# A retention layer with two gated feed-forward layers on one core: order of activations, splits, products and stores

## The chip, the core and the metric

The kernel runs on one NeuronCore of a Trainium2 chip. Five engines work there side by side, each through its own list of instructions, in the order of that list: TensorE (PE in the profile; its weight loads are shown apart as PEld), VectorE (DVE), ScalarE (ACT), GpSimd (POOL) and SyncE (SP), which here only issues transfers. An instruction starts when its engine has come to it and the semaphores that it waits for have arrived. The metric is the device time of one execution in microseconds (us), as the median of several executions.

## The reference

A retention layer (attention with a decay in place of the softmax) feeds two feed-forward layers. There are 4 batches of 576 positions, 8 heads of 64, hence 2304 tokens of 512 features; both feed-forward layers have 2048 hidden features.

```python
def _attn_ref(q, k, v):
    scores = scale * np.matmul(q, k.transpose(0, 1, 3, 2))
    Dmat = np.where(rel >= 0, gamma[:, None, None] ** rel[None, :, :], 0.0)
    return np.matmul(scores * Dmat[None], v)
def _moe_ref(x, w_in, w_out):          # layer 1
    h = x @ w_in
    g = h * np.tanh(softplus(h))
    return (g @ w_out).astype(np.float32)
def _moe2_ref(x, w_in, w_out):         # layer 2
    h = x @ w_in
    g = h * (1.0 / (1.0 + np.exp(-1.702 * h)))
    return (g @ w_out).astype(np.float32)
```

The weights of both layers come as 64-bit numbers, and all sums are wanted near float32 accuracy.

## The kernel before

**Split operands.** TensorE multiplies a shortened 32-bit format (`F32R`). Each operand of the two layers is therefore kept as a first part, rounded to that format, and a second part, the remainder; each product takes three matmuls (`PARTS`: first x first, first x second, second x first). The first part is one copy (on ScalarE through `act`, in some places on VectorE), the second part one VectorE subtraction that reads the first.

**Stage 1, retention** (to about 80 us). 20 units (batch, 128 positions) run one after another: `scores` (L738), `update` of the running state (L761), `outputs` (L786, L797), and `finish` (L811), which writes the result into the tile `X` of 512 features by 2304 columns. Between these calls stand jobs that turn the first weights of layer 1 from 64 bits into two parts (`convert`: VectorE L181, L126, L193, L234, ScalarE L117, GpSimd L197). GpSimd also scales each unit's `v` (L727). `split_x` makes the two parts of a block of columns of `X`, one 128-feature piece k at a time: first part by ScalarE for even k and by VectorE (L123) for odd k, then L333 on VectorE. In this stage it is called after the units listed in `X_UNITS`: four pieces of the first block (512 columns), then four of the side block (256 columns).

**Stage 2, layer 1** (80 to 477 us). The columns are cut into blocks; `SLOTS` lists (block, 128 hidden features) in order. The first block and the side block take turns (32 slots), then come blocks of 512 columns. At step i the program issues `up(i)` (12 matmuls, L346), `down(i - 3)` (12 matmuls, L367) and `elementwise(i)`: Mish of `h` on ScalarE into `c`, the first part of `g` on ScalarE, its second part on VectorE (L396), then jobs that convert layer 2's weights and write them to DRAM (`prepare`, on all engines). Where the next slot begins a new block, `elementwise` first calls `split_x` for all four pieces of it. The matmuls of a block's first slot are ordered so that 8 on first parts come ahead of 4 on second parts. `elementwise(0)` and `elementwise(1)` are already called in the last two units of stage 1, and the condition for a new block holds for slot 1, the side block's first.

**Stage 3, layer 2** (477 us to the end). A matrix product cut into quarters is made from seven products of sums of quarters instead of eight. Three rounds of 768 columns each have two halves. First half, "up" (L582): eight passes r, each with seven steps, one for each product p in the order `UP_ORDER`. After a step `combine` forms quarters of the hidden layer with VectorE (L428), and `after` gives a finished quarter (numbers 22, 11, 21, 12) to ScalarE for the Gelu, in place in the tile `cs` of that pass or out of a PSUM bank. Second half, "down" (L638): seven products in the order `DOWN_ORDER`, each with eight steps. A step is six matmuls in either half. `operand(i + AHEAD)`, called at the head of each step, makes the down operand that is needed three steps later: first part `g` by ScalarE, second part by VectorE (L428); the last three up steps already make operands for the first down steps. Weights come from DRAM through a ring of five tiles; `load_weights` issues each load on SyncE four tiles ahead. `leave` issues the stores of finished output quarters on SyncE.

Of the kernel before, what the change touches and what calls it, by code (L numbers as in the profile page):

```python
# [20 lines left out]
P = 128  # L21
# [17 lines left out]
BOTH = 2 * NM  # L39
# [37 lines left out]
N_ROUND = NT // (2 * TH)  # L77
NR = NM // 2
UP_ORDER = (1, 6, 5, 7, 2, 4, 3)
DOWN_ORDER = (1, 2, 5, 7, 6, 3, 4)  # L80
NP = 7
UP_STEPS = NR * NP
STEPS = 2 * UP_STEPS
# [12 lines left out]
def retention_mish_gelu_kernel(ctx: ExitStack, tc: tile.TileContext, qkv, w1, w2, gtab, gstep, vtab, cmask, out):  # L96
# [225 lines left out]
    def split_x(t, k):  # L322

        o, n = BLOCKS[t]
        if t == SIDE:
            if k % 2 == 0:
                side.append(keep.tile([P, 2, 2, WIDTH], F32R, tag=f"side{k // 2}", name="side"))
            x = side[-1][:, k % 2]
        else:
            x = keep.tile([P, 2, NB], F32R, tag=f"x{k}", name=f"x{k}")  # L330
        xs[t, k] = x
        copy(nc.vector if k % 2 else nc.scalar, x[:, 0, :n], X[:, k, o : o + n])
        return lambda: nc.vector.tensor_tensor(  # L333
            out=x[:, 1, :n], in0=X[:, k, o : o + n], in1=x[:, 0, :n].bitcast(F32), op=ALU.subtract
        )
# [63 lines left out]
    def elementwise(i, jobs=True):  # L399

        at = position if jobs else lambda *_: None
        lo, lows = None, []
        if i < len(SLOTS):
            n = BLOCKS[SLOTS[i][0]][1]
            c = keep.tile([P, NB], F32, tag="c", name="c", bufs=2)
            act(c[:, :n], hs.pop(i)[:, :n], AF.Mish)

        coming = i + 1 + (i == BOTH - 2)
        if i != BOTH - 1 and begins(coming):
            lows = [split_x(SLOTS[coming][0], k) for k in range(NK)]  # L410
        for low in lows:
            low()
        if i < len(SLOTS):
            hi, lo = split_g(i, c, n)
            hi()
        if i < BOTH or not begins(i + 1):
            at("act early", i)
        if lo:
            lo()
        if jobs and ends(i - LAG):  # L420
            evacuate(i - LAG)
        if i < BOTH or not begins(i + 1):
            at("vector", i)
            at("act late", i)
# [104 lines left out]
    def second_layer():  # L529
        pending = []  # L530

        def flush():
            while pending:
                pending.pop(0)()
# [27 lines left out]
        for s in range(N_ROUND):  # L562

            for r in range(NR):
# [2 lines left out]
                held_up, banks = {}, {}  # L567

                def after(quarter, h, where=where):
                    act(where[quarter], h, AF.Gelu_apprx_sigmoid)  # L570

                for n_p, p in enumerate(UP_ORDER):
                    i = s * STEPS + r * NP + n_p
                    if i in unit_of:
                        load_weights(unit_of[i] + len(RING) - 1)
                    operand(i + AHEAD)
                    next(coming, None)
                    banks[p] = banks[SAME[p]] if p in SAME else new_bank()[1]
                    w, x = ring.pop(i), xop[p]
# [16 lines left out]
            def to_x(e, quarter):  # L596
                return X[:, e + 2 * (quarter > 20), two(s)[quarter % 10 - 1]]

            def leave(e, quarter):
                k, half = e + 2 * (quarter > 20), two(s)[quarter % 10 - 1]  # L600
                for at, w, token in sources(half.start, TH):
                    a = half.start + at
                    nc.sync.dma_start(out=out[k * P : (k + 1) * P, token : token + w], in_=X[:, k, a : a + w])

            extra = {}

# [16 lines left out]
            for n_p, p in enumerate(DOWN_ORDER):  # L623
                for e in range(2):
                    if p == 2:
                        banks[e, p] = banks[e, 1]
                    else:
                        used[e, p], banks[e, p] = new_bank({3: used.get((e, 1)), 4: used.get((e, 7))}.get(p))
                for r in range(NR):
                    c = n_p * NR + r  # L630
                    i = s * STEPS + UP_STEPS + c
                    if i in unit_of:
                        load_weights(unit_of[i] + len(RING) - 1)
                    operand(i + AHEAD)
                    w, g = ring.pop(i), ops.pop(i)
                    for e in range(2):
                        for a, b in PARTS:
# [10 lines left out]
                for e in range(2):  # L648
# [18 lines left out]
                        at_step(at + 3, lambda e=e, u2=u2, u4=u4: add(u4, banks[e, 5], u2))  # L667
                    elif p == 3:
                        add(to_x(e, 12), banks[e, 3], sums[e, 4])
                        leave(e, 12)  # L670
                    elif p == 4:
                        add(to_x(e, 21), sums[e, 3], banks[e, 4], ALU.subtract)
                        leave(e, 21)
# [272 lines left out]
```

## Time and profile before

| what | us |
|---|---|
| median of 3 runs (839.02 to 840.79) | 840.6 |
| the profiled execution | 839.14 |
| its span, first to last instruction | 837.0 |
| TensorE busy in the span | 823.1 (98%) |
| VectorE busy | 560.0 (67%) |
| ScalarE busy | 400.0 (48%) |
| GpSimd busy | 113.9 (14%) |

The granted TensorE clock is full in all of the 40 slices of the span. A busy figure is the time covered by an engine's instructions, a wait for a shared resource inside one included; idle time of an engine counts only where the end of the program hangs on that engine. Matmuls follow each other before the last one has ended, so the start of one to the start of the next tells a delay better than the gap between them.

### The profile page before, as it was taken

To read this page: it belongs to the slowest core of one execution; us is meant where nothing else is said; L and a number is where in the kernel's file an instruction comes from. 1 tells how busy PE (TensorE), PEld (TensorE's weight loads), DVE (VectorE), ACT (ScalarE), POOL (GpSimd) and SP (SyncE) were. 2 spreads that over 40 slices of the span, in tenths; PEclk is the share of its full clock that TensorE was granted. 3 is DMA by queue.
4 is the path that set the end of the run, shared out by engine and by line. 5 is a ranking of instruction groups with operands and counts; after the bars stand their busy time and mean duration, and the time that the engine had idled before them with its cause. 6 is when DMAs were issued, how large, how long until landed. Compare 5 with 4: busy or idle time off the path is not lost.

```text
span 837.0 us, 13168 instructions
## 1 busy us (share of the span) xinstructions
PE 823.1 (98%) x4966; PEld 743.3 (89%) x4966; DVE 560.0 (67%) x1044; ACT 400.0 (48%) x738; POOL 113.9 (14%) x121
## 2 busy tenths in 40 slices
PE   8999999999999999999999999999999999999997
PEld 5887888888888888788888899999999999999997
DVE  3798765653876768687654545689655798555776
ACT  3444666663554546355533333465333565233653
POOL 2442322220322213123200000000000000000000
PEclk9999999999999999999999999999999999999999
DMA  9997800002457748668623277777877777877774
GB/s 357 368 369 283 334 20 1 1 1 100 135 187 233 239 128 251 187 201 244 194 71 95 100 254 248 245 249 248 321 259 239 247 273 241 318 253 233 247 270 155
DMA packets 96974, 175.79 MB, mean 210 GB/s; under 512 B 5520, under 2 KB 68112, under 8 KB 91408
## 3 DMA queue, kind: packets, MB, share of 16 engines
q1 hardware_dynamic: 96912, 174.97, 61.8%
q8 instruction: 39, 0.64, 0.3%
q14 instruction: 23, 0.19, 0.1%
HBM read 140.87 MB, written 34.08 MB: 209 GB/s over the span
## 4 chain that ended last, share of the span: by engine, by line
PE 86%; DVE 7%; ACT 2%; DMA 2%; issue 1%; POOL 1%; SPq 0%; ACTq 0%; POOLq 0%
PE acc L367 22%; PE h L346 21%; PE p L582 20%; PE p L638 19%; PE o L797 1%; PE sc L738 1%; PE o L786 1%; DVE x L333 1%; DMA unit<-qkv_dram 1%; DVE pm L742 1%; ACT g L117 1%; DMA stream<-cy 1%; PE ds L761 1%; DVE g L428 1%; DVE x L123 1%
## 5 line engine op out<-in xcount | busy, mean ns | idle before, releaser
L367 PE MATMUL acc<-g,w 128*128 128x512 f32 (+1 forms) x960 | 210.0, 368 | 0.0
L367 PEld LDWEIGHTS acc<-g,w 128*128 128x128 f32 x960 | 168.3, 188 | 30.4
L346 PE MATMUL h<-x,w 128*128 128x512 f32 x768 | 186.6, 391 | 1.3 <-DVE x L123 0.5
L638 PE MATMUL p<-g,ring 128*128 128x384 f32 x1008 | 178.9, 336 | 1.9 <-ACT g L117 0.9
L638 PEld LDWEIGHTS p<-g,ring 128*128 128x128 f32 x1008 | 174.4, 188 | 6.0 <-DVE g L428 2.4
L582 PE MATMUL p<-xop,ring 128*128 128x384 f32 x1008 | 175.2, 334 | 0.0
L582 PEld LDWEIGHTS p<-xop,ring 128*128 128x128 f32 x1008 | 174.8, 188 | 0.1
L346 PEld LDWEIGHTS h<-x,w 128*128 128x128 f32 x768 | 143.8, 188 | 33.5 <-DVE x L333 2.8
L396 DVE TENSOR_TENSOR g<-c,g 128x512 fp32r<-128x512 f32 x80 | 54.0, 676 | 110.1 <-ACT g L117 110.1
L117 ACT ACTIVATE g<-cs 128x384 fp32r<-128x384 f32 x168 | 86.9, 523 | 62.5 <-PE p L638 60.8
L428 DVE TENSOR_TENSOR g<-cs,g 128x384 fp32r<-128x384 f32 x168 | 91.8, 556 | 31.8 <-ACT g L117 31.0
L117 ACT ACTIVATE g<-c 128x512 fp32r<-128x512 f32 x80 | 47.2, 590 | 131.2 <-PE acc L367 131.1
L117 ACT ACTIVATE cs<-cs 128x384 f32<-128x384 f32 x72 | 37.8, 525 | 118.7 <-DVE cs L428 118.7
L197 POOL TENSOR_TENSOR cy<-cr 128x256 int32<-128x256 int32 x64 | 54.1, 865 | 184.9 <-DVE cr L193 101.6
L117 ACT ACTIVATE c<-h 128x512 f32<-128x512 f32 x80 | 44.1, 551 | 41.3 <-PE h L346 39.5
L428 DVE TENSOR_TENSOR cs<-cs 128x384 f32<-128x384 f32 x96 | 53.1, 553 | 0.8
L197 POOL TENSOR_TENSOR raw<-raw 128x512 int32<-128x512 int32 x30 | 34.3, 1144 | 97.2 <-DVE raw L193 88.9
L117 ACT ACTIVATE cr<-cr 128x512 int32<-128x512 uint32 x68 | 41.4, 663 | 1.3 <-DVE cr L181 1.3
L117 ACT ACTIVATE raw<-raw 128x512 int32<-128x512 uint32 (+1 forms) x60 | 38.0, 674 | 8.3 <-DVE raw L181 8.1
L428 DVE TENSOR_TENSOR u<-p,s 128x384 f32<-128x384 f32 x30 | 16.7, 556 | 34.9 <-PE p L582 34.9
L282 DVE TENSOR_TENSOR cy<-cy,cr 128x896 fp32r<-128x896 f32 x32 | 37.0, 1162 | 3.1 <-ACT cr L117 2.4
L428 DVE TENSOR_TENSOR cs<-p,u 128x384 f32<-128x384 f32 x48 | 26.7, 557 | 11.0 <-PE p L582 10.2
(61 smaller groups left out, 652.5 us busy)
## 6 DMA issues: line engine op xcount, KB each, us to landing
ring<-stream SPq DMA_DIRECT2D x112, 512.0 KB, 4.5
ring<-stream SPq DMA_DIRECT2D x28, 1024.0 KB, 4.6
cr<-w_dram SPq DMA_DIRECT2D x34, 512.0 KB, 4.4
unit<-qkv_dram SPq DMA_DIRECT2D x15, 1024.0 KB, 7.4
raw<-w_dram SPq DMA_DIRECT2D x30, 512.0 KB, 9.8
stream<-cr SPq DMA_DIRECT2D x32, 448.0 KB, 2.8
stream<-cy SPq DMA_DIRECT2D x32, 448.0 KB, 3.3
unit<-qkv_dram SPq DMA_DIRECT2D x6, 512.0 KB, 6.8
```

The source lines that it names most:

```text
L117: nc.scalar.activation(out=o, in_=i, func=f, scale=scale, bias=bias)
L123: eng.tensor_copy(out=o, in_=i)
L197: nc.gpsimd.tensor_tensor(out=o, in0=upper, in1=bits, op=ALU.add)
L282: nc.vector.tensor_tensor(out=y, in0=v, in1=hi.bitcast(F32), op=ALU.subtract)
L333: return lambda: nc.vector.tensor_tensor(out=x[:, 1, :n], in0=X[:, k, o : o + n], in1=x[:, 0, :n].bitcast(F32), op=ALU.subtract)
L346: nc.tensor.matmul(h[:, :n], lhsT=W[m][:, a, k * P : (k + 1) * P], rhs=xs[t, k][:, b, :n], start=((k, a, b) == order[0]), stop=((k, a, b) ...
L367: nc.tensor.matmul(acc[t, e][:, :n], lhsT=W[m][:, a, DM + e * P : DM + (e + 1) * P], rhs=g[:, b, :n],  start=(begins(i) and a == 0 and b = ...
L396: lambda: nc.vector.tensor_tensor(out=g[:, 1, :n], in0=c[:, :n], in1=g[:, 0, :n].bitcast(F32), op=ALU.subtract),
L428: eng.tensor_tensor(out=o, in0=a, in1=b, op=op)
L582: nc.tensor.matmul(banks[p], lhsT=w[:, a, k * P : (k + 1) * P], rhs=x[:, b, k], start=(p not in SAME and k == 0 and a == 0 and b == 0), st ...
L638: nc.tensor.matmul(banks[e, p], lhsT=w[:, a, e * P : (e + 1) * P], rhs=g[:, b], start=(p != 2 and r == 0 and a == 0 and b == 0), stop=(r = ...
L738: nc.tensor.matmul(sc[j][:n, p, :n], lhsT=kt[sl, p, :], rhs=qt[sl, p, :], start=True, stop=True)
```

## The change

- In layer 2, `after` only puts the Gelu on a list, and the next step issues it (`activate`), behind that step's `operand` and ahead of its matmuls.
- `elementwise` splits a coming block only for i > 0, so that the side block is split once, in `X_UNITS`.
- `split_x` makes all first parts on ScalarE.
- In `DOWN_ORDER` the last two products, 3 and 4, change places, and with them the PSUM banks that they use again.
- In the last round the last store goes to ScalarE's queue; all others stay on SyncE.

```diff
-DOWN_ORDER = (1, 2, 5, 7, 6, 3, 4)
+DOWN_ORDER = (1, 2, 5, 7, 6, 4, 3)
@@ split_x
-        copy(nc.vector if k % 2 else nc.scalar, x[:, 0, :n], X[:, k, o : o + n])
+        act(x[:, 0, :n], X[:, k, o : o + n])
@@ elementwise
-        if i != BOTH - 1 and begins(coming):
+        if i > 0 and i != BOTH - 1 and begins(coming):
@@ second_layer
+        activations = []
+        def activate():
+            while activations:
+                activations.pop(0)()
...
                 def after(quarter, h, where=where):
-                    act(where[quarter], h, AF.Gelu_apprx_sigmoid)
+                    activations.append(lambda: act(where[quarter], h, AF.Gelu_apprx_sigmoid))
...
                     operand(i + AHEAD)
+                    activate()
                     next(coming, None)
...
-            def leave(e, quarter):
+            def leave(e, quarter, queue=nc.sync):
...
-                    nc.sync.dma_start(out=out[k * P : (k + 1) * P, token : token + w], in_=X[:, k, a : a + w])
+                    queue.dma_start(out=out[k * P : (k + 1) * P, token : token + w], in_=X[:, k, a : a + w])
...
-                        used[e, p], banks[e, p] = new_bank({3: used.get((e, 1)), 4: used.get((e, 7))}.get(p))
+                        used[e, p], banks[e, p] = new_bank({4: used.get((e, 1)), 3: used.get((e, 7))}.get(p))
...
                     operand(i + AHEAD)
+                    activate()
                     w, g = ring.pop(i), ops.pop(i)
...
                         add(to_x(e, 12), banks[e, 3], sums[e, 4])
-                        leave(e, 12)
+                        leave(e, 12, nc.scalar if e and s == N_ROUND - 1 else nc.sync)
```

**Place A**, ScalarE at the end of the first round's last up pass. `cs_4822` (`cs_4811` after the change) is that pass's tile, `g2` a down operand made from an earlier pass. Before:

```order
L117 ACTIVATE s_4830<-p_4823 128x384
L117 ACTIVATE cs_4822<-cs_4822 128x384
L117 ACTIVATE g2_4863<-cs_4341 128x384
L117 ACTIVATE cs_4822<-p_4823 128x384
L117 ACTIVATE g2_4875<-cs_4408 128x384
L117 ACTIVATE cs_4822<-cs_4822 128x384
L117 ACTIVATE g2_4887<-cs_4477 128x384
L117 ACTIVATE cs_4822<-cs_4822 128x384
L117 ACTIVATE g2_4902<-cs_4546 128x384
```

After the change:

```order
L117 ACTIVATE s_4820<-p_4813 128x384
L117 ACTIVATE g2_4852<-cs_4331 128x384
L117 ACTIVATE cs_4811<-cs_4811 128x384
L117 ACTIVATE g2_4864<-cs_4397 128x384
L117 ACTIVATE cs_4811<-p_4813 128x384
L117 ACTIVATE g2_4876<-cs_4466 128x384
L117 ACTIVATE cs_4811<-cs_4811 128x384
L117 ACTIVATE g2_4891<-cs_4535 128x384
L117 ACTIVATE cs_4811<-cs_4811 128x384
```

Each of the four operand copies has moved ahead of the Gelu that stood in front of it; in the other passes ScalarE's order is the old one.

**Place B**, VectorE behind the scores of the last unit of stage 1, which is where `elementwise(0)` stands. Before:

```order
L742 TENSOR_TENSOR pm<-sc,cm 64x4x64 x2
L123 CAST side<-X 128x256 x2
L333 TENSOR_TENSOR side<-X,side 128x256 x4
L396 TENSOR_TENSOR g<-c,g 128x512
L811 TENSOR_TENSOR X<-o,gt 128x4x128
```

After the change (lines behind the diff are numbered 9 higher):

```order
L751 TENSOR_TENSOR pm<-sc,cm 64x4x64 x2
L396 TENSOR_TENSOR g<-c,g 128x512
L820 TENSOR_TENSOR X<-o,gt 128x4x128
L126 SCALAR_TENSOR_TENSOR raw<-raw 128x512
L193 TENSOR_SCALAR raw<-raw 128x512
```

The second split of the side block, six instructions here, is gone; on ScalarE two copies go with it, between the Mish into `c` and the first part of `g`.

**Place C**, VectorE ahead of the block whose first matmul starts at 336.22 us. Before:

```order
L126 SCALAR_TENSOR_TENSOR cr<-cr 128x512
L193 TENSOR_SCALAR cr<-cr 128x512
L123 CAST x_3276<-X 128x512
L123 CAST x_3280<-X 128x512
L333 TENSOR_TENSOR x_3274<-X,x_3274 128x512
L333 TENSOR_TENSOR x_3276<-X,x_3276 128x512
```

After the change:

```order
L126 SCALAR_TENSOR_TENSOR cr<-cr 128x512
L193 TENSOR_SCALAR cr<-cr 128x512
L333 TENSOR_TENSOR x_3264<-X,x_3264 128x512
L333 TENSOR_TENSOR x_3266<-X,x_3266 128x512
L333 TENSOR_TENSOR x_3268<-X,x_3268 128x512
```

The two casts have left VectorE; ScalarE makes four copies in a row there instead of two. The same holds at the three other block starts, and in stage 1 four single casts go over to ScalarE.

## Rows read from the trace of the kernel before

**Rows 1.** The page, parts 1 and 5: busy time; last field idle time ahead.

```profile
PE 823.1 (98%) x4966; PEld 743.3 (89%) x4966; DVE 560.0 (67%) x1044; ACT 400.0 (48%) x738; POOL 113.9 (14%) x121
...
L582 PE MATMUL p<-xop,ring 128*128 128x384 f32 x1008 | 175.2, 334 | 0.0
```

**Rows 2.** Busy time by stretch: PE, PEld, DVE, ACT, POOL, clock, DMA, GB/s.

```profile
40.00:57.00 17.00, 16.76 (x258) 14.45 (x255) 16.78 (x27) 8.66 (x17) 9.59 (x9) 1.00 0.97 366
57.00:69.00 12.00, 10.56 (x150) 8.72 (x147) 11.90 (x20) 5.31 (x11) 4.07 (x4) 1.00 0.97 361
```

**Rows 3.** Timeline, GpSimd and VectorE at an odd piece's split in stage 1.

```profile
55.15 3.73 POOL L727 TENSOR_TENSOR unit<-unit,vt 64x512 f32<-64x512 f32 x3
...
56.71 1.26 DVE L123 CAST x<-X 128x512 fp32r<-128x512 f32 x1
...
58.01 1.41 DVE L333 TENSOR_TENSOR x<-X,x 128x512 fp32r<-128x512 f32 x1
```

**Rows 4.** Timeline, TensorE and ScalarE at the side block's first slot.

```profile
78.46 1.09 PE L797 MATMUL o<-pm,unit 128*64 128x128 f32 x16
80.56 1.85 PE L346 MATMUL h<-side,w 128*128 128x256 f32 x12 [1.01 <-ACT side L117]
...
80.10 0.71 ACT L117 ACTIVATE side<-X 128x256 fp32r<-128x256 f32 x2
```

**Rows 5.** Timeline, TensorE at two block starts: `up`, then the next `down`.

```profile
292.15 3.41 PE L346 MATMUL h<-x,w 128*128 128x512 f32 x12
295.39 2.91 PE L367 MATMUL acc<-g,w 128*128 128x512 f32 x12
...
336.22 0.61 PE L346 MATMUL h<-x,w 128*128 128x512 f32 x2
...
341.29 2.90 PE L367 MATMUL acc<-g,w 128*128 128x512 f32 x12
```

**Rows 6.** Timeline, VectorE, GpSimd and ScalarE at the second of these starts.

```profile
336.90 0.76 DVE L123 CAST x<-X 128x512 fp32r<-128x512 f32 x2
...
337.57 3.33 DVE L333 TENSOR_TENSOR x<-X,x 128x512 fp32r<-128x512 f32 x4
...
337.61 2.13 POOL L197 TENSOR_TENSOR cy<-cr 128x256 int32<-128x256 int32 x2 [2.87 <-DMA stream<-cy]
...
334.19 1.14 ACT L117 ACTIVATE x<-X 128x512 fp32r<-128x512 f32 x2
```

**Rows 7.** The chain that ended last, in order of time: start, us, what.

```profile
303.74 2.72 PE h L346 x12
...
477.71 55.16 PE p L582 x318
...
596.08 55.13 PE p L582 x318
```

**Rows 8.** Timeline, ScalarE and VectorE where the first round turns from up to down.

```profile
536.89 0.53 ACT L117 ACTIVATE cs<-cs 128x384 f32<-128x384 f32 x1 [1.09 <-DVE cs L428]
...
537.86 0.56 DVE L428 TENSOR_TENSOR g<-cs,g 128x384 fp32r<-128x384 f32 x1 [1.00 <-ACT g L117]
```

**Rows 9.** Waits from 477 us on: who, for whom, us, times, longest.

```profile
PEld p L638 <- ACT s L117: 1.1, 3, 0.4
```

**Rows 10.** Timeline, VectorE and SyncE (SPq) at the end.

```profile
832.28 1.08 DVE L428 TENSOR_TENSOR X<-u,p 128x384 f32<-128x384 f32 x2 [2.52 <-PE p L638]
...
832.86 1.77 SPq L603 DMA_DIRECT2D out_dram<-X  x4
```

**Rows 11.** DMA issues: engine, count, KB each, median us from issue to landing.

```profile
ring<-stream SPq DMA_DIRECT2D x28, 1024.0 KB, 4.6
...
out_dram<-X SPq DMA_DIRECT2D x12, 192.0 KB, 3.1
...
out_dram<-X SPq DMA_DIRECT2D x12, 64.0 KB, 2.8
...
cm<-cmask_dram SPq DMA_DIRECT2D x1, 64.0 KB, 4.8
```

## The prediction

> **What bounds the kernel now.** Read the busy line first [rows 1]. TensorE is busy for 823.1 us of a span of 837.0, so 13.9 us is all that it idles, and the other engines have room over the whole. The work of TensorE is the same after the change, matmul for matmul; a gain can come only out of the places where it stands still, and out of the end of the program, after its last matmul. So the second view is the idle time by stretch and, inside the stretches, the timeline of TensorE and of the engine that it waits for. Four kinds of place come out, and the change touches each.
>
> *Retention.* From 40 to 57 us TensorE is busy for 16.76 of 17.00 us, from 57 to 69 us for 10.56 of 12.00 [rows 2]: 0.24 and 1.44 us idle, 1.68 together. VectorE is busy for 16.78 and 11.90 of the same stretches, so it is VectorE that TensorE waits for there, though only just.
>
> *The side block's first slot.* The unit's last product starts at 78.46 and takes 1.09 us; the next matmuls start at 80.56, after 1.01 us of idle time that a copy of ScalarE ends [rows 4].
>
> *Block starts.* Twelve matmuls take 2.72 us undisturbed [rows 7]. At two block starts they take 295.39 - 292.15 = 3.24 and 341.29 - 336.22 = 5.07 us [rows 5]: 0.52 and 2.35 us lost, 2.87 together.
>
> *Layer 2.* A round takes 596.08 - 477.71 = 118.37 us [rows 7]. It holds 672 matmuls; 318 of them in a row take 55.16 us [rows 7], 0.1735 each, which makes 116.57. So 1.80 us of a round are lost. The up half idles for 0.0 us [rows 1], so the loss lies in the down half. There, the waits behind the copies `s` (first to second product, three times in all) come to 1.1 us or 0.37 a round [rows 9]; the other 1.43 lie where up turns into down. Three rounds: 4.3 us.
>
> **The Gelu a step later.** At place A the four operand copies move ahead of four Gelus. What they stand behind now: a Gelu waits 1.09 us for VectorE's quarter, runs 0.53 us, and only then comes the operand's first part, whose second part VectorE waits for, 1.00 us idle [rows 8]; VectorE's next quarter stands behind that second part in its order, and the next Gelu behind that quarter. The two engines pass the work to and fro, and the operand of the third down step is late. None of these operands needs the last pass: its source is a quarter of passes 0 to 3, finished long ago. With the copies first, the copy for down step 0 can run before 534 us, and each later one as soon as the Gelu of the step before has gone. By hand, with 0.53 us for each copy, 0.56 for each subtraction or quarter and rows 8 for their starts: the operand of down step 2 is whole near 536.6 instead of 538.4, that of step 3 near 537.7, against matmuls wanted at about 537.9 and 538.9. That is over a microsecond ahead, so I take the whole loss: 3 x 1.43 = 4.3 us. What is queued behind the waiting instruction now is the Gelu itself, later by one copy; VectorE's two subtractions on that quarter stand a step further on, and their result is an operand many steps later. In the 21 other passes ScalarE's order doesn't change, so nothing is bought or paid. Bounds: 3.0 if one of the two late steps stays late, 5.4 (three times 1.80) if even the `s` waits go.
>
> **The side block split once.** The two copies on ScalarE and six instructions on VectorE go [place B]. The copies run from 80.10 for 0.71 us [rows 4], behind the Mish of slot 0; TensorE waits for them alone. The first split, made units earlier, holds the same numbers. Next in line for these matmuls is only TensorE itself, done at 79.55. Gain 80.56 - 79.55 = 1.0 us; bounds 0.6, if the bank's former reader comes late, and 1.1.
>
> **First parts on ScalarE, at block starts.** At the start at 336.22, VectorE runs two casts in 0.76 us and then four subtractions in 3.33 us, beside two GpSimd additions [rows 6]; the last matmuls wait for the last subtraction. With the casts gone the subtractions begin 0.67 us earlier (337.57 - 336.90), GpSimd's start is set by a transfer and stays, so the last one ends about 0.6 us earlier. ScalarE now makes four copies of 0.57 us (1.14 / 2) from 334.19 on, to 336.5; the fourth is wanted six matmuls after 336.22, at 337.6. The 8 matmuls on first parts then wait for nothing, those on second parts still do: 0.6 of 2.35 us. At 292.15 only 0.52 us are lost and two casts are worth at least 0.67: all of it. The other two starts show no loss worth a row and count as zero. Together 1.1 us; bounds 0.5, if GpSimd takes back what the casts leave, and 2.87.
>
> **First parts on ScalarE, in retention.** Four casts leave VectorE, where they stand next to GpSimd's work. One took 1.26 us with GpSimd busy beside it and the subtraction behind it 1.41 [rows 3]; undisturbed, two casts took 0.76 us [rows 6], 0.38 each. So some 0.9 us of such a cast is a wait. Three of the four come before 69 us. If the subtraction takes the cast's place behind the same GpSimd instruction, the cast and one whole turn of waiting go, 1.26 us a time, more than the 1.68 us of idle time by 69 us; if the wait passes on to the subtraction in full, 0.38 us a time. I take most of it, 1.5 of 1.68, since in rows 3 cast and subtraction each lose a turn and one of the two instructions is gone; bounds 0.8 and 1.68. ScalarE, which takes the copies, is busy for 8.66 of 17 and 5.31 of 12 us there [rows 2]; a copy may hold up a copy of the state behind it, whose reader comes a unit later.
>
> Here the Trainium skill speaks against the change. In its page "SBUF — State Buffer", section "Who interferes with whom", it says that VectorE and GpSimd share one pair of ports under an exclusive lock held for a whole instruction, and that a VectorE instruction with two SBUF inputs, which L333 is, contends for it as a cast does. By that rule L333 meets the lock in the cast's place. The long L333 in rows 3 agrees with the rule; whether a turn is saved, no row shows. What this would give as a time is the first rival.
>
> **Products swapped, two store queues.** VectorE's last two additions take 1.08 us from 832.28, and SyncE then issues four stores in 1.77 us from 832.86, 0.44 each [rows 10]; the span ends at 837.0. The last product after the change has one store for each half e, since quarter 12 of the last round is one stretch of tokens and quarter 21 two. The one for e = 1 goes to ScalarE's queue, free since its last operand, as soon as the addition ends at 833.36; issued by 833.8 instead of 834.63. It is 192 KB instead of 64, which costs 3.1 against 2.8 us to land [rows 11]. Gain 0.83 - 0.3 = 0.5 us. No row shows a transfer issued by ScalarE. Bounds: a gain of 0.8, or a loss of 1.5, if that queue's first transfer lands as much later as the 64 KB load at the program's start did, 4.8 against 2.8 us [rows 11]. In the first two rounds it is the other way round: four stores instead of two now stand at the round's end, ahead of a 1 MB weight load on SyncE, which leaves 2 x 0.44 = 0.9 us later. It is issued four ring tiles, at least eight steps of 1.04 us, ahead and lands in 4.6 us [rows 11]; the 3.7 us between cover it. Cost nothing; if the cover is gone, up to 0.9 us in each of two rounds.
>
> **The sum.** 4.3 + 1.0 + 1.1 + 1.5 + 0.5 = 8.4 us. The profiled execution took 839.14, so it would take 830.7. The median of the runs, 840.6, lies 1.5 above it; the same difference taken from it gives **832.2 us**.
>
> **Rivals.** *The lock passes on* (0.22). The subtraction takes over the cast's wait, in retention and at the block starts: 0.8 instead of 1.5 and 0.5 instead of 1.1, so 7.1 us in all, 833.5. For it: the long L333 in rows 3. Against it: the pair lost two turns where one is left.
>
> *The turn of layer 2 gains half* (0.12). Operands come in time for step 2, but the two subtractions of the last pass, which wait for a Gelu that is now later, stand ahead of the next operands on VectorE and make a later step late; half of 4.3 goes: 834.4. For it: VectorE takes these steps one by one and waits 1.00 us in rows 8. Against it: the microsecond and more worked out above.
>
> *The change does not do what it says* (0.04). Each stall only moves to what is late next (weights from DRAM in layer 2, transfers in retention), and at most a microsecond is left: 840.
>
> *Slower* (0.04). One mechanism: ScalarE's Gelu, issued a step later, holds up each of the 24 up passes, since the next pass's `s` copy stands behind it and TensorE's banks behind that. A Gelu takes 0.53 us [rows 8]; one in each pass costs 12.7 us, against 8.4 gained: 844.9. It decides from 8.4 / 24 = 0.35 us a pass. Against it: up idles for 0.0 us now [rows 1], and ScalarE's order in those passes is unchanged.
>
> **How the numbers follow.** The forecast has 0.58. The runs of one kernel spread over 1.8 us, so 0.2% (1.7 us) is about what a measurement of it can tell from no change. The forecast's own bounds run from 3.4 us gained (3.0 + 0.6 + 0.5 + 0.8 - 1.5) to 11.9 (5.4 + 1.1 + 2.87 + 1.68 + 0.8), and neither end needs all its parts at once; with the first two rivals the range is 828.8 to 835.4, the lower end with the faster of the shown runs as the base. The first three cases are faster: 0.92; within 0.2%: 0.04; slower: 0.04.
>
> **What the profile of the changed kernel would show.** The waits of L638's weight loads on VectorE and ScalarE's `g` should be gone, those on `s` stay at about 1.1 us, and a round should take 117.0 us. TensorE should run from the last unit's product into the side block's first slot without a gap. The starts at 292 and 336 us should take 2.7 and about 4.5 us. Retention should show under 0.4 us of idle time between 40 and 69 us. The last store should be ScalarE's and the time from the last matmul to the end 0.5 us shorter. I am wrong if L638 then waits for a weight load, if a block start waits for ScalarE, or if L742 still keeps TensorE waiting.

## The result, and the profile after

| what | before | after |
|---|---|---|
| median of four runs (lowest to highest), us | 840.02 (839.02 to 840.79) | 828.53 (828.15 to 830.33) |
| ratio, 95% interval | | 0.987 (0.9855 to 0.9886) |
| the profiled execution, us | 839.14 | 828.15 |
| its span, us | 837.0 | 826.2 |

The changed kernel is 1.3% faster. The forecast of 832.2 us had the direction and most of the mechanisms right and the size too small: 828.53 lies 0.3 us under the low end of its range in us, and inside it as a share of the time before (828.8 of 840.6 is 0.986). Lines of the changed kernel behind the first edits are numbered up to 9 higher (L582 is L590, L638 is L647, L738 is L747, L797 is L806, L727 is L736).

**Retention.** Busy time by stretch, the answer to [rows 2] (PE, PEld, DVE, ACT, POOL, clock, DMA, GB/s):

```profile
40.00:57.00 17.00, 17.00 (x262) 14.83 (x264) 16.92 (x25) 9.78 (x20) 9.91 (x9) 1.00 0.99 380
57.00:69.00 12.00, 11.93 (x180) 10.37 (x179) 11.93 (x23) 6.12 (x14) 5.65 (x6) 1.00 0.97 359
```

TensorE's idle time has fallen from 1.68 to 0.07 us; VectorE is as full as before. The timeline tells more. TensorE of the kernel before, one unit's scores to the next but one:

```profile
60.74 1.16 PE L738 MATMUL sc<-unit 64*128 64x128 f32 x16
61.84 0.69 PE L761 MATMUL ds<-unit 128*64 128x64 f32 x16
62.61 0.43 PE L797 MATMUL o<-pm,unit 128*64 128x128 f32 x2
...
63.21 1.09 PE L797 MATMUL o<-pm,unit 128*64 128x128 f32 x14 [0.17 <-DVE pm L742]
64.22 1.16 PE L738 MATMUL sc<-unit 64*128 64x128 f32 x16
...
69.38 1.16 PE L738 MATMUL sc<-unit 64*128 64x128 f32 x16
```

The same units after the change, and the first matmuls of layer 1:

```profile
59.34 1.16 PE L747 MATMUL sc<-unit 64*128 64x128 f32 x16
60.43 0.69 PE L770 MATMUL ds<-unit 128*64 128x64 f32 x16
60.95 1.54 PE L806 MATMUL o<-pm,unit 128*64 128x128 f32 x16
...
62.42 1.16 PE L747 MATMUL sc<-unit 64*128 64x128 f32 x16
...
66.53 1.16 PE L747 MATMUL sc<-unit 64*128 64x128 f32 x16
...
70.34 3.01 PE L346 MATMUL h<-x,w 128*128 128x512 f32 x12
```

From scores to scores the first of these units fell from 3.48 to 3.08 us, 0.40 less, while the rows before show only 0.25 us of gaps in it (0.17 ahead of the 14 matmuls, 0.08 ahead of the two): the rest of the stall lies inside the shown durations. The next unit fell from 5.16 to 4.11. Over the whole of retention, from the third unit's scores (12.90 before, 12.62 after) to layer 1's first matmul (73.20, 70.34), 60.30 us became 57.72: **2.58 us**. Another 0.28 us lie ahead of that, where both kernels wait for the first transfers; in the profiles of all kernels this start lies between 12.48 and 12.90, so it is no work of the edits.

**The side block's first slot.** TensorE after the change, against [rows 4]:

```profile
75.60 1.09 PE L806 MATMUL o<-pm,unit 128*64 128x128 f32 x16
76.63 1.70 PE L346 MATMUL h<-side,w 128*128 128x256 f32 x12
```

The gap is gone. From layer 1's first matmul to the side block's it is 6.29 us instead of 7.36 (80.56 - 73.20): 1.07, and 0.15 more up to the next slot, **1.22**.

**Block starts.** TensorE and VectorE after, against [rows 5] and [rows 6]:

```profile
288.04 2.88 PE L346 MATMUL h<-x,w 128*128 128x512 f32 x12
290.76 2.88 PE L367 MATMUL acc<-g,w 128*128 128x512 f32 x12
...
331.56 2.20 PE L346 MATMUL h<-x,w 128*128 128x512 f32 x9
...
332.30 3.33 DVE L333 TENSOR_TENSOR x<-X,x 128x512 fp32r<-128x512 f32 x4
...
336.02 2.94 PE L367 MATMUL acc<-g,w 128*128 128x512 f32 x12
```

The first start takes 2.72 us instead of 3.24; the second 336.02 - 331.56 = 4.46 instead of 5.07. A third, at 420.40 after and 425.63 before, takes 5.44 us to the next slot instead of 5.68. Slot to slot (to the next slot's first `up` matmul, over the `down` between) the three gain 0.55, 0.57 and 0.24: **1.36**.

**Layer 2.** Chain of waits after, against [rows 7], and the one wait that is left at L647, against [rows 9]:

```profile
472.24 58.26 PE p L590 x336
530.51 7.29 PE p L647 x42
538.89 50.19 PE p L647 x288
589.08 58.24 PE p L590 x336
```

```profile
PEld p L647 <- ACT s L117: 1.1, 3, 0.4
```

A round takes 589.08 - 472.24 = 116.84 us instead of 118.37. The down half now starts right behind the 336 matmuls of up; before, the chain broke after 318. 1.53 a round, **4.6** in all.

**The end.** VectorE and the two queues, against [rows 10]:

```profile
822.23 1.08 DVE L428 TENSOR_TENSOR X<-p,u 128x384 f32<-128x384 f32 x2 [2.52 <-PE p L647]
822.81 0.33 SPq L611 DMA_DIRECT2D out_dram<-X  x1
823.34 0.38 ACTq L611 DMA_DIRECT2D out_dram<-X  x1
```

From VectorE's last two additions to the end of the span: 826.2 - 822.23 = 3.97 us instead of 837.0 - 832.28 = 4.72: **0.75**.

Together 0.28 + 2.58 + 1.22 + 1.36 + 4.6 + 0.75 = 10.8 us, the difference of the spans.

### The profile page after: what moved, and what is told of

It reads as the page before. It is cut to its first block, busy times and chain, and to the rows that moved or that the text cites. A ratio compares the mean times of both kernels' runs of the same rounds, so it can differ in the third digit from the quotient of the medians.

```text
span 826.2 us, 13183 instructions
## 1 busy us (share of the span) xinstructions
PE 817.4 (99%) x4966; PEld 743.2 (90%) x4966; DVE 554.5 (67%) x1026; ACT 405.9 (49%) x748; POOL 113.9 (14%) x121
## 4 chain that ended last, share of the span: by engine, by line
PE 91%; DVE 5%; DMA 1%; issue 1%; POOL 1%; ACT 0%; SPq 0%; POOLq 0%; DVEq 0%; ACTq 0%
PE acc L367 22%; PE h L346 22%; PE p L590 21%; PE p L647 21%; PE o L806 2%; PE o L795 1%; PE sc L747 1%; DMA unit<-qkv_dram 1%; DVE pm L751 1%; DVE x L333 1%; PE ds L770 1%; POOL cy L197 1%; DMA stream<-cy 0%; DVE w L234 0%; DVE X L820 0%
## 5 line engine op out<-in xcount | busy, mean ns | idle before, releaser
L647 PE MATMUL p<-g,ring 128*128 128x384 f32 x1008 | 176.0, 334 | 0.2
L647 PEld LDWEIGHTS p<-g,ring 128*128 128x128 f32 x1008 | 174.5, 188 | 1.3 <-ACT s L117 1.1
L590 PE MATMUL p<-xop,ring 128*128 128x384 f32 x1008 | 175.2, 334 | 0.0
L590 PEld LDWEIGHTS p<-xop,ring 128*128 128x128 f32 x1008 | 174.8, 188 | 0.1
L396 DVE TENSOR_TENSOR g<-c,g 128x512 fp32r<-128x512 f32 x80 | 55.6, 695 | 113.2 <-ACT g L117 113.2
L282 DVE TENSOR_TENSOR cy<-cy,cr 128x896 fp32r<-128x896 f32 x32 | 37.8, 1186 | 2.6 <-ACT cr L117 2.1
```

What stands on the lines that cost most here:

```text
L282: nc.vector.tensor_tensor(out=y, in0=v, in1=hi.bitcast(F32), op=ALU.subtract)
L396: lambda: nc.vector.tensor_tensor(out=g[:, 1, :n], in0=c[:, :n], in1=g[:, 0, :n].bitcast(F32), op=ALU.subtract),
L590: nc.tensor.matmul(banks[p], lhsT=w[:, a, k * P : (k + 1) * P], rhs=x[:, b, k], start=(p not in SAME and k == 0 and a == 0 and b == 0), st ...
L647: nc.tensor.matmul(banks[e, p], lhsT=w[:, a, e * P : (e + 1) * P], rhs=g[:, b], start=(p != 2 and r == 0 and a == 0 and b == 0), stop=(r = ...
```

## The experiments

**Theory:** each of the five edits takes away the stall that the prediction names, on a stretch of its own, and the sizes add. Rivals: the casts' wait passes on to the subtractions, or only the idle time between matmuls can be won; the Gelu's move gains half; the second queue brings nothing. The first four runs make one part of the change alone in the kernel before.

| kernel | median, us | ratio to before, 95% |
|---|---|---|
| Gelu later, alone | 835.31 | 0.9947 (0.9934 to 0.996) |
| first parts on ScalarE, alone | 835.96 | 0.9954 (0.9941 to 0.9967) |
| side block split once, alone | 838.61 | 0.9991 (0.9983 to 0.9999) |
| swap and two queues, alone | 838.95 | 0.9989 (0.998 to 0.9998) |
| (before beside these four) | 839.59 | |
| changed, stage 1's casts back on VectorE | 831.17 | 0.9905 (0.989 to 0.9919) |
| changed, Gelu later in last passes only | 828.6 | 0.9872 (0.9857 to 0.9887) |
| changed, all stores on SyncE | 828.95 | 0.9875 (0.986 to 0.989) |
| changed, product 5 between 1 and 2 | 828.2 | 0.9868 (0.9852 to 0.9885) |
| (before beside these four) | 839.47 | |
| changed, once more | 828.31 | 0.9864 (0.9851 to 0.9878) |
| changed, down ahead at block starts | 826.5 | 0.9841 (0.9828 to 0.9855) |
| changed, both of these | 826.0 | 0.9837 (0.9823 to 0.985) |
| before, four casts made twice | 841.08 | 1.0012 (1.0003 to 1.0021) |
| (before beside these four) | 839.83 | |

### The Gelu a step later, alone

The three hunks of the diff in `second_layer` that make, fill and empty `activations`; nothing else.

> The kernel before with the delayed Gelu alone; all else as before. Theory (the late operands at the turn from up to down are the loss, and putting the copies ahead of the Gelus takes all but the s waits away): a round goes from 118.37 us to 116.8 to 117.0, the weight loads of L638 wait no more for VectorE or for ScalarE's g but still 1.1 us in all for s, and the time falls by 4.1 to 4.7 us. Rival (the turn gains half, because the last pass's own subtractions then stand ahead of the next operands): a round of 117.7, 2.1 us less. Rival (a Gelu held back costs something in every up pass): a round longer than 118.4. Stage 1 and stage 2 as before within 0.2 us.

Chain of waits:

```profile
478.07 58.26 PE p L588 x336
536.34 7.29 PE p L645 x42
544.72 50.23 PE p L645 x288
594.95 58.24 PE p L588 x336
```

A round takes 594.95 - 478.07 = 116.88 us (L588 and L645 are L582 and L638 here); the waits on VectorE and on `g` are gone, those on `s` stay at 1.1 us. 4.3 us less by the medians. The rival that gains half is out, and so is the one that loses. Stage 2 did not stay as before within 0.2 us: its block start at GpSimd's work took 0.65 us longer in this profile, of which more below.

### The same in the last pass only

```diff
-                    activations.append(lambda: act(where[quarter], h, AF.Gelu_apprx_sigmoid))
+                    gelu = lambda: act(where[quarter], h, AF.Gelu_apprx_sigmoid)
+                    if r == NR - 1:
+                        activations.append(gelu)
+                    else:
+                        gelu()
```

> The changed kernel with the Gelu held back a step in the last up pass of each round only; in the 21 other passes it is issued at once, as before. Theory (only the turn from up to down matters): a round of 116.8 us and a time within 0.3 us of the changed kernel. Rival (holding the Gelu back costs a little in every pass, or gains a little): the up half of a round, 58.26 us for 336 matmuls, differs by more than 0.1 us.

828.6 us, the first round's up half 58.26 us, a round 116.84. In the 21 other passes the later Gelu neither costs nor brings anything, as the prediction had it from ScalarE's unchanged order there.

### First parts on ScalarE: alone, and taken back in stage 1

```diff
-        copy(nc.vector if k % 2 else nc.scalar, x[:, 0, :n], X[:, k, o : o + n])
+        act(x[:, 0, :n], X[:, k, o : o + n])
```

> The kernel before with the first parts all on ScalarE alone; the side block is still split twice. Theory (each VectorE cast beside GpSimd costs the chain of retention a whole turn of the shared port, and stalled matmuls hide part of that inside their own durations): from the scores of the third unit to the last unit's scores, start to start, 2.3 to 2.7 us less, which is more than the 1.68 us of idle time between matmuls of this stretch; block starts together 1.3 to 1.5 us less; total 3.6 to 4.2 us less. Rival (idle time between matmuls is all there is to win): at most 1.7 in retention, 2.8 to 3.2 in all. Rival (the lock passes on to the subtraction): 0.8 and 0.5, 1.3 in all. The first slot of the side block may lose up to 0.7 us, since ScalarE then makes four copies there instead of two; a round of layer 2 stays at 118.4.

Retention, start to start as above: 70.14 - 12.55 = 57.59 us, 2.71 less than before. The block starts of this profile: 0.56, 0.19 and 0.24, 0.99 together, under the 1.3 to 1.5 expected (why the second differs from the 0.57 above stands below). 3.6 us less by the medians. Then the changed kernel with only stage 1's four casts back on VectorE:

```diff
-        act(x[:, 0, :n], X[:, k, o : o + n])
+        copy(nc.vector if k % 2 and slot[0] == 0 else nc.scalar, x[:, 0, :n], X[:, k, o : o + n])
```

> The changed kernel with one thing put back: in stage 1 the first parts of odd pieces are cast on VectorE again (four casts); the block starts of stage 2 keep ScalarE. Theory (each such cast costs the chain a turn of the shared port): from the third unit's scores to the first matmul of layer 1, start to start, 2.4 to 2.7 us more than in the changed kernel, and as much in the whole. Rival (only the idle time between matmuls counts): at most 1.7 us more. Rival (the subtraction takes the wait over): 0.8 us more. Everything from the side block's first slot on as in the changed kernel.

Retention 73.08 - 12.72 = 60.36 us, 2.64 more than after; the medians differ by 2.6 us (831.17 against 828.6 beside it). Both ways round, the four casts are worth more than the 1.68 us between matmuls, and the rivals with 1.7 and 0.8 are out.

The sizes come out of VectorE's rows, at the three places that lie ahead of layer 1's first matmul. Before (the second place is [rows 3]):

```profile
42.12 1.26 DVE L123 CAST x<-X 128x512 fp32r<-128x512 f32 x1
43.42 0.69 DVE L333 TENSOR_TENSOR x<-X,x 128x512 fp32r<-128x512 f32 x1
...
64.80 1.13 DVE L123 CAST side<-X 128x256 fp32r<-128x256 f32 x1
65.96 1.15 DVE L333 TENSOR_TENSOR side<-X,side 128x256 fp32r<-128x256 f32 x1
```

After:

```profile
41.83 1.52 DVE L333 TENSOR_TENSOR x<-X,x 128x512 fp32r<-128x512 f32 x1
...
62.99 1.26 DVE L333 TENSOR_TENSOR side<-X,side 128x256 fp32r<-128x256 f32 x1
```

From the start of the cast to the end of the subtraction VectorE spent 1.99, 2.71 and 2.31 us; the subtraction alone takes 1.52, 1.53 and 1.26. That is 2.70 us less of VectorE, waits included, against 2.58 of retention (2.71 with these copies alone on ScalarE).

### What the subtraction does in the cast's place

GpSimd and VectorE at the second of the four places, after the change (before: [rows 3], cast 1.26 and subtraction 1.41):

```profile
54.53 3.99 POOL L736 TENSOR_TENSOR unit<-unit,vt 64x512 f32<-64x512 f32 x3
...
56.09 1.53 DVE L333 TENSOR_TENSOR x<-X,x 128x512 fp32r<-128x512 f32 x1
```

The same kernel, run once more:

```profile
54.48 3.54 POOL L736 TENSOR_TENSOR unit<-unit,vt 64x512 f32<-64x512 f32 x3
...
56.05 2.53 DVE L333 TENSOR_TENSOR x<-X,x 128x512 fp32r<-128x512 f32 x1
```

> The changed kernel once more, as the neighbour of the next two. Expected: 828.2 to 829.0 us. The block start at which GpSimd works beside the split (matmuls from 331.56 us on in the changed kernel's profile) has taken between 4.4 and 5.3 us in five profiles of kernels with these copies on ScalarE and between 5.1 and 6.1 in four with VectorE's casts; theory: its length hangs on when VectorE comes to the split, which moves with the transfers, and it falls again into 4.4 to 5.3 us.

The subtraction does wait beside GpSimd, as the cast did: 1.53 us, where the same subtraction took 0.69 once GpSimd was done (the last row of the next timeline). By the Trainium skill's rule ("SBUF — State Buffer", "Who interferes with whom") it must, and the traces agree; that rule alone does not say how many turns are lost. Here the pair of 1.26 + 1.41 = 2.67 us became one instruction of 1.53 or 2.53. Which of the two it is differs between executions of one program: the instruction starts 1.6 us into GpSimd's run of three in both, and in one execution it is done at 57.62, ahead of the end of GpSimd's run (58.52), in the other at 58.58, behind it (58.02). Of eight profiles with the copies on ScalarE, five have 57.6 to 58.0 us of retention and three, this one (58.61) among them, 58.6 to 59.0; the three are those in which this subtraction took 2.5 us, and in the five it took 1.5 to 1.6. In this profile VectorE spends 1.70 us less at the three places than before, and retention is 1.69 shorter. Of five profiles with VectorE's casts, four have 60.3 to 60.4 and one (the swap and two queues, alone) 61.2. By these means the edit is worth 60.5 - 58.15 = 2.3 us, and the 2.58 of the two profiles shown is a little more than that. 828.31 us, as expected; the block start at GpSimd's work took 339.89 - 332.52 - 2.72 = 4.65 us, inside its band.

Then the cast made twice, in the kernel before:

```diff
-                    split_x((0, SIDE)[k // NK], k % NK)()
+                    t = (0, SIDE)[k // NK]
+                    low = split_x(t, k % NK)
+                    if k % 2:
+                        o1, n1 = BLOCKS[t]
+                        nc.vector.tensor_copy(out=xs[t, k % NK][:, 0, :n1], in_=X[:, k % NK, o1 : o1 + n1])
+                    low()
```

> The kernel before with each of the four casts of VectorE in retention made twice (the second writes the same numbers again). Theory (a cast beside GpSimd's work costs the chain a turn of the shared port, some 0.65 us on the mean, because 2.6 us went with four): retention another 1.5 to 2.6 us longer. Rival (a cast costs its undisturbed 0.38 us, and the rest of the wait is there whatever VectorE does): 1.5 us or less. Rival (idle time of VectorE takes it up): under 0.5. All else as before.

Timeline at the same place:

```profile
55.36 3.54 POOL L727 TENSOR_TENSOR unit<-unit,vt 64x512 f32<-64x512 f32 x3
...
56.93 2.26 DVE L123 CAST x<-X 128x512 fp32r<-128x512 f32 x1
59.22 0.43 DVE L850 CAST x<-X 128x512 fp32r<-128x512 f32 x1
59.68 0.69 DVE L333 TENSOR_TENSOR x<-X,x 128x512 fp32r<-128x512 f32 x1
```

Retention is 1.5 us longer than in the profile of before and the median 1.25 us: on the border between theory and rival, so this run does not tell them apart by its total. Its rows do say why a turn per instruction was too simple. Here the first cast waited for the rest of GpSimd's run, and the second cast and the subtraction behind it ran undisturbed. VectorE's time at the three places grew by 0.45, 0.73 and 0.33 us, 1.51 together, and retention by 1.51. So what a cast costs here is neither a turn nor its bare 0.38 us, but what it adds to the stretch from the start of the pair to its end: where VectorE comes while GpSimd works, it may get in before the end of the run (1.53) or only behind it (2.26, 2.53), and what follows then waits no more.

### The side block split once, alone

```diff
-        if i != BOTH - 1 and begins(coming):
+        if i > 0 and i != BOTH - 1 and begins(coming):
```

> The kernel before with the side block split once alone. Theory: the matmuls of the side block's first slot start right behind the last unit's product, 1.0 to 1.2 us earlier against the slot before, and the time falls by 1.0 to 1.3 us, all of it there. Rival (something else is late there, a bank or the weights): a gap of 0.4 us or more stays and at most 0.6 us is won. Everything after that slot as before within 0.2 us.

```profile
78.10 1.09 PE L797 MATMUL o<-pm,unit 128*64 128x128 f32 x16
79.12 1.70 PE L346 MATMUL h<-side,w 128*128 128x256 f32 x12
```

No gap. From layer 1's first matmul (72.83 here, 73.20 before) to the side block's, 6.29 us instead of 7.36, and to the slot behind, 9.37 instead of 10.59: 1.22. 1.0 us by the medians. The theory holds, but not the expectation's last sentence: the block start at GpSimd's work took 1.1 us longer in this profile than in that of before.

### That block start: 1.1 us between profiles of like code

The start at 336 us, slot to slot less the 2.72 us of `down` between, in five profiles with VectorE's casts: 5.09 (before), 5.74, 6.20, 5.36, 5.48; in seven with ScalarE's copies: 4.52 (after), 4.90, 4.64, 4.91, 4.50, 5.35, 4.65. The means are 5.57 and 4.78, **0.8 us** apart. The single profiles spread over about a microsecond on either side, since the split stands in VectorE's order behind additions of GpSimd, which the rows show waiting for a transfer in five of the twelve profiles and for VectorE's own L282 or L396 in the others, and comes 0.7 to 1.8 us after the start's first matmul.

VectorE in the profile with the side block split once, at this start:

```profile
336.41 1.17 DVE L123 CAST x<-X 128x512 fp32r<-128x512 f32 x2
...
337.50 2.90 DVE L333 TENSOR_TENSOR x<-X,x 128x512 fp32r<-128x512 f32 x4
```

Here the casts carry the wait beside GpSimd (1.17 us instead of the 0.76 of [rows 6]) and the subtractions do not (2.90 instead of 3.33); so it is in four of the five profiles with VectorE's casts. The whole split takes 3.99 to 4.00 us in all five all the same, and 3.33 in all seven with ScalarE's copies. Take from each of the twelve lengths the time until VectorE comes and the split's own time, and 0.41 to 0.46 us are left. So at this start the wait does pass on in full from the casts to the subtractions, the edit itself is worth 0.67 us, the casts' undisturbed time, and all the rest of the spread is when VectorE comes.

### Two queues

The swap and the queue alone, in the kernel before (the `DOWN_ORDER`, `leave` and `new_bank` hunks):

> The kernel before with the last two products swapped and the last store on ScalarE's queue alone. Theory: the end, from the last matmul to the last instruction, gets 0.5 to 0.75 us shorter, rounds stay at 118.4 us, and nothing else moves: 0.5 to 0.75 us less in all. Rival (the weight load behind four stores comes late): the first two rounds get up to 0.9 us longer each and the kernel comes out slower by up to 1.2 us. Rival (ScalarE's queue lands its first store late): the end gets up to 1.5 us longer.

From the last additions to the end of the span 837.0 - 833.00 = 4.0 us, 0.72 less; a round 596.78 - 478.39 = 118.39 us, as before. So the four stores ahead of a weight load cost nothing. 0.6 us by the medians, although in this profile retention took 0.9 us longer. Then the changed kernel with every store on SyncE:

```diff
-                        leave(e, 12, nc.scalar if e and s == N_ROUND - 1 else nc.sync)
+                        leave(e, 12)
```

> The changed kernel with all stores on SyncE; the last two products stay swapped. From the last matmul to the end the kernel before took 4.23 us and the changed kernel 3.49. Theory (half of the gain is the swap, since two stores instead of four then stand at the end, and half is the second queue): 3.8 to 4.0 us. Rival (the queue is all of it): 4.2. Rival (the swap is all of it): 3.5. All else as in the changed kernel.

Timeline:

```profile
822.10 1.08 DVE L428 TENSOR_TENSOR X<-p,u 128x384 f32<-128x384 f32 x2 [2.52 <-PE p L647]
822.68 0.86 SPq L611 DMA_DIRECT2D out_dram<-X  x2
```

The span ends at 826.0, 3.9 us behind the additions, as in the changed kernel. My theory of halves falls: in the profiles the swap is all of it (the medians, 828.95 against 828.3 to 828.6 for the changed kernel and its like, are too close to say). It leaves two stores at the end instead of four, SyncE has issued the first (0.33 us) before the second addition is done, and there is no queue to get round.

### What is left

**Product 5 between products 1 and 2**, in the changed kernel:

```diff
-DOWN_ORDER = (1, 2, 5, 7, 6, 4, 3)
+DOWN_ORDER = (1, 5, 2, 7, 6, 4, 3)
```

> The changed kernel with the second and third product of the down half in the other order: product 5, which uses banks of its own, comes between product 1 and product 2, which adds to product 1's banks and so must wait for ScalarE's copy s of them. Theory (the 0.33 us that a round still loses are this wait and nothing else): no waits of the down half's weight loads on s, a round of 116.5 us instead of 116.84, 0.9 to 1.1 us less in all than the changed kernel. Rival (the bank or the operands for product 5 come late instead): a round of 116.8 or more.

Chain of waits:

```profile
473.27 58.26 PE p L590 x336
531.53 58.24 PE p L647 x336
589.77 58.24 PE p L590 x336
```

A round is 116.50 us, and nothing of its 672 matmuls waits: the 0.33 us were the `s` waits. Three of them are 1.0 us; the median shows 0.3 to 0.4 of it, which at this size it cannot confirm, and in this profile retention and the block start at GpSimd's work together took 1.1 us more than in the profile of after.

**Down ahead at block starts**, in the changed kernel:

```diff
-                up(i)
-            if i >= LAG:
+                if i >= BOTH and begins(i):
+                    down(i - LAG)
+                    up(i)
+                else:
+                    up(i)
+                    if i >= LAG:
+                        down(i - LAG)
+            elif i >= LAG:
                 down(i - LAG)
```

> The changed kernel with one thing added: where a slot begins a new block in the second part of layer 1, the 12 matmuls of the earlier slot's down product, which need nothing of the new block, are issued ahead of the slot's up matmuls instead of behind them. Theory (what is left of that start's loss, 1.7 us in the changed kernel, is the wait for VectorE's four subtractions, and 2.7 us of other matmuls cover it): the 24 matmuls of the two products take 5.5 to 6.1 us there instead of 7.24, and the kernel 1.2 to 2.0 us less. Rival (a later up makes a later slot's Mish and down product late): the loss comes back within the next three slots, and nothing is won.

VectorE and TensorE at the start in question:

```profile
330.15 5.60 PE L367 MATMUL acc<-g,w 128*128 128x512 f32 x24
...
334.07 3.33 DVE L333 TENSOR_TENSOR x<-X,x 128x512 fp32r<-128x512 f32 x4
...
335.59 3.79 PE L346 MATMUL h<-x,w 128*128 128x512 f32 x16
```

24 `down` matmuls run in a row and 24 `up` matmuls behind them, without a wait (the view ends after 16 of these). From the slot ahead (327.43) to the slot behind (338.31) it is 10.88 us, four times 2.72: nothing is lost any more, and no later slot gives it back. 1.8 us by the medians. Then **both**:

> The changed kernel with both additions: the down product ahead at block starts, and product 5 between products 1 and 2 in the down half of layer 2. Theory (they lie on different stretches of the same chain and add): 2.2 to 3.0 us less than the changed kernel, 825.5 to 826.3 us, a round of 116.5 us and no block start above 6.1 us for its 24 matmuls. Rival: less than 1.5 us.

826.0 us, 2.3 less than the changed kernel beside it: 0.9837 of the kernel before, and the fastest of all. A round is 116.50 us here too (first matmul at 471.78, the next round's at 588.28), so the parts add on the chain; the run's own retention was of the longer kind (59.03 us).

## Why the prediction was right, and why too small

- **The Gelu a step later** (4.3): right, 4.6. The `s` waits stayed, as said; the 1.43 a round were 1.53, because the round without stalls was put at 116.57 us from one row of 318 matmuls, and two rows of 336 make it 2 x 58.24 = 116.48.
- **The side block split once** (1.0): right, 1.07, and 0.15 in the slot behind, which the step did not look at.
- **Block starts** (1.1): right for the two that were named, 0.55 and 0.57. The third, counted as zero because it showed no loss worth a row, lost 0.24 and gave it back. The 0.6 at GpSimd's start was well sized: 0.67 is the casts' time there. But GpSimd's start, which the step put down to a transfer and held fixed, is set by one in the profile of before alone; in the 13 others VectorE's own L193 releases it, 0.22 us behind the start of the split, so the additions move with the split. The size came out because the split's time shrank by the casts' time either way.
- **Retention** (1.5): **the step that failed.** It took the idle time between matmuls, 1.68 us, as a cap on the gain, although the section on the profile says itself that starts tell a delay better than gaps. Start to start the gain is 2.58, with both single experiments at 2.6 to 2.7. The bounds 0.8 and 1.68 should have been bounds on starts. The working from [rows 3] had a larger number, a whole turn of 1.26 us at three places, and was cut down to the cap; uncut it would have been 3.8 us and too much. VectorE's time fell by 0.47, 1.18 and 1.05 us at the three places.
- **The lock passes on** (the rival): half right. In retention the subtraction does wait in the cast's place, yet about a turn goes at two of the three places, and at the second of them (1.18) only in the executions in which the subtraction gets in early; else 0.18. At GpSimd's block start the rival's mechanism holds in full: the wait passes on to the subtractions, and only the casts' time of 0.67 us was won.
- **The tail** (0.5): 0.75, for a partly wrong reason. The second queue, to which the step gave the gain, brings nothing; that there are two stores behind the last product instead of four brings all. The last store is issued 1.11 us after the additions begin (823.34 - 822.23) instead of 1.93, a gain of 0.82; its 192 KB take 1.92 us to land where the last 64 KB took 1.65, so the 0.3 charged for that came; and 0.2 less lie between landing and the end of the span.
- **Stores ahead of the weight load** (nothing): right, rounds unchanged.
- **Slower** (0.04): out; the up half takes 58.26 us whether the Gelu is held back in all eight passes or in one.
- **The base.** 840.6 was the median of three runs; four gave 840.02, and the 23 beside the first experiments 839.59. Some 0.6 to 1.0 us of the miss is in this. The range's low end has the same base: 828.8 is 840.6 less the 11.85 of all upper bounds, and not, as the prediction has it, reckoned from the faster run; from 839.02 these bounds reach 827.2, and 828.53 would lie inside.

By stretch the miss is 1.08 in retention, 0.3 in layer 2, 0.28 at the program's start, 0.26 at block starts, 0.25 at the end and 0.22 at the side block: 2.4 of the 2.55 us between the 830.7 forecast for the profiled execution and its 828.15. The single parts of the first four runs add up to 4.3 + 3.6 + 1.0 + 0.6 = 9.5 us by the medians, against 11.5 for the whole. By stretch of the profiles they add up to 4.5 + 2.7 + 1.0 + 1.2 + 0.7 = 10.1 of 10.5 (the 10.8 less the program's start). The 2 us between the medians are not explained; the intervals of the four ratios, some 0.7 to 1.1 us either way each, allow them.

## What to carry to other kernels

Size a stall from the start of one matmul to the start of the next over the whole stretch, not from the idle time between shown ends, which here held 1.7 of some 2.6 us; where another engine is the limit of the stretch, the change in that engine's own time, waits included, gives the gain (2.70 and 1.70 us for 2.58 and 1.69). Look at several profiles of one kernel where two engines' work meets, for the meeting can fall differently in each execution, and one profile shows one of several lengths. And where a stage waits at its turn, look for work of a finished stage that can stand ahead of the waiting instruction in the same engine's order: the copies ahead of the Gelu, the down product ahead of the up product and product 5 ahead of product 2 are the same edit three times, and in the traces each took its stall away whole.

## What was not expected of the hardware

- One subtraction beside a run of three GpSimd instructions took 1.53 us in one execution and 2.53 in another of the same program, and retention with it 57.7 or 58.6 us.
- A store issued by ScalarE, the first on its queue, landed 1.9 us after its issue, as SyncE's second store did in the kernel with one queue (1.88); a queue's first use had no price of its own here. The row of the DMA issues after the change (engine, count, KB, us from issue to landing):

```profile
out_dram<-X ACTq DMA_DIRECT2D x1, 192.0 KB, 1.9
```
